# Hash attention and MLP mixer: keys and channels on the partitions, two heads side by side on the array, attention first and the mixer after it

## The chip, the cores and the metric

The kernel runs on one core of a Trainium2 chip. A core has a matrix engine (TensorE, PE in the profile; its loads of stationary operands are listed apart as PEld), VectorE (DVE), ScalarE (ACT), GpSimd (POOL), and SyncE (SP), which here only starts transfers. Matrix products read SBUF and write PSUM, which has eight banks of 512 float32 per partition. The metric is the time of one execution on the device, in microseconds.

## The reference

For 4 batches, 8 heads, 768 tokens and a head size of 64, each query attends to the keys whose six hash bits equal its own. The heads' outputs, side by side, are the input x (768 x 512) of a mixer with 256 hidden token units and 1536 hidden channels.

```python
q_bits = (einsum('bhsd,dk->bhsk', q, proj) > 0)      # k_bits likewise; 6 bits give a bucket
mask = q_bucket[:, :, :, None] == k_bucket[:, :, None, :]
scores = where(mask, (q @ k.T) / 8, -1e9)
scores = scores - max(scores, axis=-1, keepdims=True)
attn = exp(scores)
attn = attn / (sum(attn, axis=-1, keepdims=True) + 1e-9)
x = (attn @ v)                                       # (B, H, S, D) -> (B, S, H*D)

h = maximum(x.transpose(0, 2, 1) @ w_tok1, 0) @ w_tok2
u = x + h.transpose(0, 2, 1)
out = u + maximum(u @ w_ch1, 0) @ w_ch2
```

All is float32; the mixer's weights arrive as float64. q, k and v are normal numbers times 0.1.

## The kernel before

The work is written as steps, and a scheduler orders each engine's instructions from them. `run` interleaves two step generators: `attention_steps` of a batch beside `mixer_steps` of the batch before it (beside the first batch it is `double_weight_steps`, which converts the float64 weights in 20 chunks). The mixer of the last batch runs alone at the end.

A pair of heads shares the 128 partitions, 64 dimensions each. `prepare` turns q and k on TensorE, so that dimensions lie on the partitions (line 197, the helper `turn`), and computes the hash bits (line 215). `scores` takes 128 queries at a time: queries on the partitions, 768 keys along the row, one 1024-wide PSUM tile a head. A bfloat16 product of the scaled bits (line 233, 7 rows) adds 0 where all bits agree and a huge negative number elsewhere; the float32 product of q and k (line 239, 64 rows of the array a head) follows. VectorE takes the row's maximum (line 249), GpSimd scales it (253), ScalarE exponentiates and sums (256). `attend` turns the 128 x 768 weights, six blocks a head (197, copied out by 199 and 201), multiplies them with v (275: 128 queries stationary, 64 columns moving), and divides (280 to 282).

A float32 product is two instructions on TensorE, so counts in the profile are twice the program's; a transpose or a bfloat16 product is one.

The mixer has its token products at lines 319 and 330, a turn of u (197 again), and the channel products at 347 (384 columns) and 359 (512 columns). A weight chunk is a transfer and seven operations: four on VectorE (148, 152, 157, 160), two on GpSimd (163, 166), one more on VectorE (170).

Of the kernel before, what the change touches and what calls it, by code (L numbers as in the profile page):

```python
# [12 lines left out]
chip. Weights that come as float32 are loaded as they are.  # L13
"""
# [11 lines left out]
U32 = mybir.dt.uint32  # L26
I64 = mybir.dt.int64
ALU = mybir.AluOpType
ACT = mybir.ActivationFunctionType


@with_exitstack
def kernel(
    ctx: ExitStack,
    tc: tile.TileContext,
    q: bass.AP,
    k: bass.AP,
    v: bass.AP,
    proj: bass.AP,
# [8 lines left out]
    B, H, S, D = q.shape  # L48
    NB = proj.shape[1]
    DM = H * D  # L50
# [3 lines left out]
    NP = H // 2  # L54
# [3 lines left out]
    assert D == 64 and S == 6 * P and DM == 512 and NB <= 8 and H % 2 == 0  # L58
    assert DTOK % P == 0 and DCH % P == 0
    HALF = S // 2  # L60
    RH = NR // 2

    SCALE = 0.125
    MASKED = -1e9 / SCALE
    BIG = 2.0**62

    const = ctx.enter_context(tc.tile_pool(name="const", bufs=1))
    pool = ctx.enter_context(tc.tile_pool(name="sb", bufs=2))
    psum = ctx.enter_context(tc.tile_pool(name="ps", bufs=2, space=bass.MemoryType.PSUM))

# [4 lines left out]
    projblk = const.tile([P, 64], F32, name="projblk")  # L75
    nc.vector.memset(projblk, 0.0)
    for i in range(2):
        nc.sync.dma_start(out=projblk[D * i : D * i + D, 32 * i : 32 * i + NB], in_=proj)
    # Row NB has the bit -1/2 on both sides: -NB * BIG there cancels NB agreeing bits.
    bitscale = const.tile([64, 1], F32, name="bitscale")  # L80
    nc.gpsimd.memset(bitscale, BIG)
    for i in range(2):
        nc.gpsimd.affine_select(
            out=bitscale, in_=bitscale, compare_op=ALU.not_equal, fill=-NB * BIG,
            base=-(32 * i + NB), pattern=[[0, 1]], channel_multiplier=1,
        )

# [1 line left out]
    W1 = const.tile([P, NR, DTOK], F32, name="W1")  # L89
    W2 = const.tile([P, NJ, NR, P], F32, name="W2")  # L90
    WC1 = const.tile([P, NCB, DCH], F32, name="WC1")
    WC2 = const.tile([P, NHT, DM], F32, name="WC2")
# [7 lines left out]
    def words(w):  # L100
        return w.bitcast(U32) if double else w

    w1v = words(w_tok1).rearrange("(p r) c -> p (r c)", r=NR)
    w2v = words(w_tok2).rearrange("(j p) c -> p j c", p=P)
    wc1v = words(w_ch1).rearrange("(j p) c -> p j c", p=P)
    wc2v = words(w_ch2).rearrange("(t p) c -> p t c", p=P)
    W1f = W1.rearrange("p r c -> p (r c)")

    chunks = []
    for n in range(NR * DTOK // NW):  # L110
        chunks.append((w1v[:, NE * NW * n : NE * NW * (n + 1)], W1f[:, NW * n : NW * (n + 1)], None))
    for j in range(NJ):
        chunks.append((w2v[:, j], W2[:, j].rearrange("p r s -> p s r"), (S // NR, NR)))
    for j in range(NCB):
        for n in range(DCH // NW):
            chunks.append((
                wc1v[:, j, NE * NW * n : NE * NW * (n + 1)], WC1[:, j, NW * n : NW * (n + 1)], None,
            ))
    PER = 256
    for n in range(DM // PER):  # L120
        for t in range(NHT // 3):
            chunks.append((
                wc2v[:, 3 * t : 3 * t + 3, NE * PER * n : NE * PER * (n + 1)],
                WC2[:, 3 * t : 3 * t + 3, PER * n : PER * (n + 1)], (3, PER),
            ))

    def plain_weight_steps():
        for src, dst, shape in chunks:
            if shape == (S // NR, NR):
                raw = pool.tile([P, NW], F32, name="raw", tag="big", bufs=4)  # L130
                nc.gpsimd.dma_start(out=raw, in_=src)
                nc.vector.tensor_copy(dst, raw.rearrange("p (s r) -> p s r", r=NR))
            else:
                nc.gpsimd.dma_start(out=dst, in_=src)
            yield

    def double_weight_steps():
        for src, dst, shape in chunks:
            raw = pool.tile([P, NW, 2], U32, name="raw", tag="big", bufs=4)
            flat = raw.rearrange("p n w -> p (n w)")  # L140
            if len(src.shape) == 3:
                flat = flat.rearrange("p (t c) -> p t c", t=src.shape[1])
            nc.gpsimd.dma_start(out=flat, in_=src)
# [3 lines left out]
            # float32 with the high word's 20 bits of mantissa  # L147
# [8 lines left out]
            # the low word, in units of the number's signed power of two  # L156
# [3 lines left out]
            nc.vector.scalar_tensor_tensor(  # L160
                unit, lo, 2.0**-52, unit, op0=ALU.mult, op1=ALU.mult,
            )
            nc.gpsimd.tensor_tensor(big, big, unit, op=ALU.add)  # L163
            # what lies below float32's normal numbers is 0
            size = lo.bitcast(F32)
            nc.gpsimd.tensor_tensor(size, hi.bitcast(F32), hi.bitcast(F32), op=ALU.mult)  # L166
            if shape is not None:
                big = big.rearrange("p (a b) -> p a b", a=shape[0])
                size = size.rearrange("p (a b) -> p a b", a=shape[0])
            nc.vector.scalar_tensor_tensor(  # L170
                dst, size, LEAST * LEAST, big, op0=ALU.is_ge, op1=ALU.mult,
            )
            yield

# [1 line left out]
    def load_pair(b, hp):  # L176
        tiles = []
        for name, t in (("q", q), ("k", k)):
            nat = pool.tile([P, NR, 2, D], F32, name=f"{name}n", tag=f"{name}n")
            for i in range(2):  # L180
                nc.sync.dma_start(
                    out=nat[:, :, i], in_=t[b, 2 * hp + i].rearrange("(p r) d -> p r d", r=NR),
                )
            tiles.append(nat)
# [7 lines left out]
    def turn(dst, blocks, on_act):  # L192
# [3 lines left out]
        for i, block in enumerate(blocks):  # L196
            nc.tensor.transpose(ps[:, P * i : P * i + P], block, ident)  # L197
# [93 lines left out]
    def load_ahead(n):  # L291
        if n < len(pairs):
            loaded[pairs[n]] = load_pair(*pairs[n])
# [123 lines left out]
```

## Time and profile before

| | |
|---|---|
| three runs | 1546.4, 1555.5, 1544.23 us; median 1546.4 |
| span of the profiled execution, first to last instruction | 1543.2 us |
| what lies around the span | 3.2 us to the median, 1.0 us to the fastest run; the page has no time of its own for the profiled execution beside the span |
| busy, share of the span | PE 1482.8 us (96%), PEld 893.6 (58%), DVE 503.3 (33%), ACT 342.8 (22%), POOL 121.2 (8%) |
| transfers | 41.92 MB, mean 27 GB/s |

A busy share is an average over stages, and a matmul's end in the profile is modelled: an instruction is shown somewhat longer than the distance to the next one. What a matmul costs in a stream is read from the starts of its neighbours, or from a group's busy time divided by its count in a window where nothing else runs. PEclk is the share of TensorE's full clock that was granted.

### The profile page before, as it was taken

The page shows a single profiled execution, that of the slowest core. Times are in us where ns is not written, and L with a number is a line of the kernel's source. Part 1 is how long each engine was busy: PE and PEld are TensorE (multiplying, and loading weights), DVE is VectorE, ACT ScalarE, POOL GpSimd, SP SyncE. Part 2 cuts the span into 40 slices and gives each one's busy share as a digit, 9 for nine tenths or more (in the row PEclk, how much of TensorE's full clock was granted, in tenths as well). Part 3 has the DMA queues.
Part 4 walks back from the last instruction along what each step waited for, and adds up shares of the span by engine and source line. Part 5 has one row for each costly group of instructions (what it writes and reads, how often), then busy time and mean ns, then how long its engine had stood idle before and what let it go on. Part 6 is the DMA issues. An engine that isn't in the chain of part 4 may idle for free.

```text
span 1543.2 us, 15967 instructions
## 1 busy us (share of the span) xinstructions
PE 1482.8 (96%) x6560; PEld 893.6 (58%) x6560; DVE 503.3 (33%) x1141; ACT 342.8 (22%) x729; POOL 121.2 (8%) x261
## 2 busy tenths in 40 slices
PE   5999999899999999999999999999999999999998
PEld 2666656565656556654665556654566555655554
DVE  4455454623432323223432322223432232221000
ACT  1112122212332212212232122212223122211110
POOL 3223232300000000000000000000000000000000
PEclk7566565759999999999999999999999999999999
DMA  7122121101010101001010101001010000000000
GB/s 214 41 62 73 54 80 41 31 1 31 1 31 1 38 15 29 3 14 38 1 31 0 38 14 31 1 15 38 0 31 1 7 15 0 1 14 7 7 14 21
DMA packets 61609, 41.92 MB, mean 27 GB/s; under 512 B 51296, under 2 KB 55392, under 8 KB 61536
## 3 DMA queue, kind: packets, MB, share of 16 engines
q1 hardware_dynamic: 58144, 25.18, 6.1%
q0 software_dynamic: 3392, 15.73, 3.0%
q8 instruction: 51, 0.84, 0.2%
q14 instruction: 22, 0.18, 0.0%
HBM read 34.61 MB, written 6.29 MB: 27 GB/s over the span
## 4 chain that ended last, share of the span: by engine, by line
PE 89%; DVE 6%; issue 2%; POOL 1%; ACT 1%; DMA 0%; DVEq 0%; POOLq 0%; ACTq 0%
PE acc L275 19%; PE c L347 16%; PE c L359 16%; PE sc L239 15%; PE trp L197 11%; PE sc L233 5%; PE hp L215 3%; DVE e L249 3%; PE h L330 3%; PE t L319 3%; DVE eT L201 1%; POOL raw L166 0%; POOL tmp L163 0%; ACT e L256 0%; DMA raw<-in_moe_w_tok 0%
## 5 line engine op out<-in xcount | busy, mean ns | idle before, releaser
L275 PEld LDWEIGHTS acc<-vn,eT 128*128 128x128 f32 x2304 | 313.3, 220 | 7.7 <-issue 6.2
L275 PE MATMUL acc<-vn,eT 128*128 128x64 f32 x2304 | 317.3, 302 | 0.0
L249 DVE TENSOR_SCALAR_CACHE_REDUCE e<-sc 128x768 f32<-128x768 f32 x192 | 176.4, 955 | 347.8 <-PE sc L239 342.8
L256 ACT ACTIVATE e<-e,low 128x768 f32<-128x768 f32 x192 | 179.1, 933 | 461.5 <-POOL low L253 461.1
L359 PE MATMUL c<-WC,r 128*128 128x512 f32 x576 | 259.0, 595 | 0.0
L347 PE MATMUL c<-uT,WC 128*128 128x384 f32 x768 | 256.1, 489 | 0.0
L239 PE MATMUL sc<-kT,qT 64*128 64x512 f32 (+1 forms) x768 | 254.0, 587 | 0.0
L197 PE MATMUL trp<-ident,e 128*128 128x128 f32 x1152 | 194.6, 310 | 18.6 <-DVE eT L201 12.4
L197 PEld LDWEIGHTS trp<-ident,e 128*128 128x128 f32 x1152 | 140.7, 155 | 107.3 <-issue 46.0
L347 PEld LDWEIGHTS c<-uT,WC 128*128 128x128 f32 x768 | 143.3, 190 | 93.0 <-issue 1.9
L359 PEld LDWEIGHTS c<-WC,r 128*128 128x128 f32 x576 | 105.3, 190 | 111.9 <-issue 109.8
L239 PEld LDWEIGHTS sc<-kT,qT 64*128 64x128 f32 x768 | 94.0, 209 | 98.6 <-issue 93.9
L199 ACT COPY eT<-trp 128x384 f32<-128x384 f32 x192 | 90.1, 469 | 265.0 <-PE trp L197 261.8
L201 DVE COPY eT<-trp 128x384 f32<-128x384 f32 x192 | 106.4, 555 | 110.4 <-PE trp L197 110.1
L253 POOL TENSOR_SCALAR low<-top 128x1 f32<-128x1 f32 x192 | 42.1, 220 | 1101.9 <-DVE e L249 1101.8
L352 ACT ACTIVATE r<-c 128x384 f32<-128x384 f32 x96 | 47.1, 490 | 315.0 <-PE c L347 315.0
L233 PE MATMUL sc<-kb,qb 7*128 7x512 bf16 (+1 forms) x384 | 93.2, 356 | 18.8 <-DVE e L249 14.5
L282 DVE TENSOR_TENSOR x<-acc,den 128x128 f32<-128x128 f32 x96 | 27.9, 291 | 234.1 <-PE acc L275 234.1
L233 PEld LDWEIGHTS <-qb 7*128 7x128 bf16 x384 | 22.6, 93 | 117.6 <-issue 114.6
L366 DVE TENSOR_TENSOR o<-c,x 128x512 f32<-128x512 f32 x24 | 16.6, 691 | 177.4 <-PE c L359 177.4
L163 POOL TENSOR_TENSOR tmp<-tmp 128x768 f32<-128x768 f32 x20 | 36.1, 1803 | 109.0 <-DVE tmp L160 102.3
L330 PE MATMUL h<-r,W 128*128 128x512 f32 x96 | 44.2, 601 | 0.0
(45 smaller groups left out, 550.4 us busy)
## 6 DMA issues: line engine op xcount, KB each, us to landing
raw<-in_moe_w_ch POOLq DMA_DIRECT2D x16, 768.0 KB, 4.8
qn<-in_q SPq DMA_DIRECT2D x32, 192.0 KB, 3.3
kn<-in_k SPq DMA_DIRECT2D x32, 192.0 KB, 3.4
vn<-in_v SPq DMA_DIRECT2D x16, 384.0 KB, 3.2
out<-o SPq DMA_DIRECT2D x24, 256.0 KB, 2.0
raw<-in_moe_w_tok POOLq DMA_DIRECT2D x4, 768.0 KB, 7.5
projblk<-in_proj SPq DMA_DIRECT2D x2, 1.5 KB, 4.9
```

The costliest lines, as they stand in the source:

```text
L197: nc.tensor.transpose(ps[:, P * i : P * i + P], block, ident)
L199: nc.scalar.copy(dst, ps[:, : P * n])
L201: nc.vector.tensor_copy(dst, ps[:, : P * n])
L233: nc.tensor.matmul(ps[i][:, ks], qb[32 * i : 32 * i + NB + 1, qs], kb[32 * i : 32 * i + NB + 1, ks], start=True, stop=False,)
L239: nc.tensor.matmul(ps[i][:, ks], qT[D * i : D * i + D, qs], kT[D * i : D * i + D, ks], start=False, stop=True,)
L249: nc.vector.tensor_scalar(e, ps[i][:, :S], MASKED, None, op0=ALU.max, op1=ALU.max, accum_out=top[:, i : i + 1],)
L256: nc.scalar.activation(e, e, ACT.Exp, bias=low[:, i : i + 1], scale=SCALE, accum_out=sums[:, i : i + 1],)
L275: nc.tensor.matmul(acc[:, D * i : D * i + D], eT[i][:, P * c : P * c + P], vn[:, i, c], start=(i == 0 and c == 0), stop=(c == NR - 1), ski ...
L330: nc.tensor.matmul(ps, W2[:, j, r], r1[:, j], start=(j == 0), stop=(j == NJ - 1),)
L347: nc.tensor.matmul(ps[:, :HALF], WC1[:, cb, P * t : P * t + P], uT[cb // 2][:, cb % 2, sl], start=(cb == 0), stop=(cb == NCB - 1),)
L352: nc.scalar.activation(r2t, ps[:, :HALF], ACT.Relu)
L359: nc.tensor.matmul(ps, r2[t][:, P * c : P * c + P], WC2[:, t], start=(t == 0), stop=(t == NHT - 1),)
```

## The change

The program is rewritten. The host now hands in q and k already turned (`in_qk`, dimensions on the partitions), v in key chunks and a turned v as well; the output leaves with channels on the partitions and is turned back by the host.

- Scores have keys on the partitions: a tile is 128 keys x 2 heads x 384 queries, two PSUM banks. The two heads use rows 0 to 63 and 64 to 127 of the array. The bits are spread by small transfers to the same 64 rows a head, padded with zeros, so bits and scores have one shape.
- No maximum is subtracted: the exponential reads PSUM directly (masked scores become 0). `look` records the largest |q| and |k|; where it is above 2, a flag makes the kernel run `careful_attention` and the mixer a second time behind a branch.
- The weights need no turning: v is stationary (128 keys x 64), the exponentials move (384 queries), and the two heads write partitions 0 to 63 and 64 to 127 of one bank (columns of the array).
- Sums over keys: GpSimd and VectorE add the six tiles of a half (`collect`), a product with ones sums over the partitions, and `divide` also puts the mean of v where no key matched.
- x stays turned (`XT`, all batches). The mixer turns it back for the first token product (`turn`), keeps u with channels on the partitions, and takes 512 tokens at a time in `channels`.
- All attention comes first; then all of the mixer, with pools of its own. Within both, TensorE's order is the order in which the program is written; the scheduler orders the other engines. The channel weights are loaded and converted at the start of the mixer, 4 chunks a batch; the token weights during the first pairs of heads.

```diff
+        def product(t, c, first):                       # in scores(n, half, chunks)
+            for i in range(2):
+                rows = slice(D * i, D * i + D)
+                nc.tensor.matmul(                       # L232
+                    sc[c][:, i, :HALF], t[rows, 1, P * c : P * c + P], t[rows, 0, qs],
+                    start=first, stop=not first)
...
+                for c in chunks:
+                    product(qkt, c, True)
+                    product(bits, c, False)
+            for c in chunks:
+                e = pool.tile([P, 2, HALF], F32, name="e", tag="e", bufs=11)
+                nc.scalar.activation(e, sc[c][:, :, :HALF], ACT.Exp, scale=SCALE)   # L249
...
+        def weigh(n, acc, es, chunks):
+            for c, e in zip(chunks, es):
+                for i in range(2):
+                    nc.tensor.matmul(                   # L257
+                        acc[D * i : D * i + D, :HALF], vn[:, i, c], e[:, i],
+                        start=(c == 0), stop=(c == NR - 1))
...
+        def collect(es):
+            nc.gpsimd.tensor_tensor(a, es[0], es[1], op=ALU.add)       # L265
+            nc.gpsimd.tensor_tensor(a, a, es[2], op=ALU.add)           # L266
+            nc.vector.tensor_tensor(d, es[3], es[4], op=ALU.add)       # L268
+            nc.vector.tensor_tensor(d, d, es[5], op=ALU.add)           # L269
+            nc.vector.tensor_tensor(d, d, a, op=ALU.add)               # L270
...
+        def divide(n, half, num, es):
+            ps = psum.tile([P, 512], F32, name="sums", tag="sm", bufs=1)   # hashes uses "sm" too
+            for i in range(2):
+                nc.tensor.matmul(ps[D * i : D * i + D, :HALF], ones, es[:, i], ...)   # L278
+            # none, den, reciprocal, num on VectorE (L280, L282, L285, L286), XT on GpSimd (L290)
...
+        for n, half, g in groups:          # 16 pairs x 2 halves of the queries x 2 groups of 3 key chunks
+            es = scores(n, half, range(GR * g, GR * g + GR))
+            if held is not None:
+                step(held)                 # weigh of the group before; divide and collect by halves
+            held = (n, half, g, es)
+            if half == 0 and g == 0:
+                load(n + 3)
+                look(n + 1)                # L195 on VectorE, L198 on ScalarE
+            if half == 1 and g == 0 and n % 2 == 1:
+                hashes(n + 1)              # L207: bits of the next two pairs; 8 transfers, L218
+            if weights and n >= 2 and half == 0 and g == 1:
+                weights.pop(0)()           # a chunk of the token weights
...
+        turn(0)                            # mixer: L430
+        for b in range(B):
+            some_weights(4)                # L133 to L155, as lines 143 to 170 were
+            if b + 1 < B:
+                turn(b + 1)
+            mix1(b)                        # L440
+            if b:
+                mix2(b - 1)                # L452, its adds L458 on VectorE
+        mix2(B - 1)
...
+        for tt in range(B * S // TT):      # 6 x 512 tokens
+            channels(tt)                   # L466 (c1), L476 (c2)
...
+    run(attention)
+    run(mixer, True)
+    flag = nc.values_load(unsafe, min_val=0, max_val=1)
+    with tc.If(flag > 0):
+        run(careful_attention)
+        run(mixer, False)
```

On TensorE, in the middle of an attention stage, there stood before (sc are the scores, qb and kb the bits, trp the turned blocks of the exponentials e, acc the attention's output):

```order
L197 MATMUL trp<-ident,e 128x128 x6
L233 LDWEIGHTS qb
L233 MATMUL sc<-kb,qb 128x512
L233 LDWEIGHTS qb
L233 MATMUL sc<-kb,qb 128x256
L239 MATMUL sc<-kT,qT 128x512
L197 MATMUL trp<-ident,e 128x128 x6
L275 MATMUL acc<-vn,eT 128x64 x6
```

and there stands now, for one group (its last of three key chunks is shown, then the products with v of the group before and the sums):

```order
L232 MATMUL sc<-qk 128x384 x2
L232 LDWEIGHTS bits_98
L232 MATMUL sc<-bits_98 128x384
L232 LDWEIGHTS bits_98
L232 MATMUL sc<-bits_98 128x384
L257 MATMUL acc<-e,vn 64x384 x6
L278 MATMUL sums<-esd,ones 64x384 x2
```

The two heads' products were often apart (a single line 239 between bits and transposes); now each pair follows its partner, the transposes are gone, and the 64-column products have become 384 columns wide.

On VectorE, where the first weight chunks are converted, there stood before a chunk spread among the maxima and copies of the attention:

```order
L148 TENSOR_SCALAR tmp<-raw 128x768
L281 RECIPROCAL den<-den 128x2
L152 SCALAR_TENSOR_TENSOR tmp<-raw,tmp 128x768
L282 TENSOR_TENSOR x<-acc,den 128x128
L157 TENSOR_SCALAR tmp<-tmp 128x768
L160 SCALAR_TENSOR_TENSOR tmp<-raw,tmp 128x768
L249 TENSOR_SCALAR e,top<-sc 128x768 x2
L201 COPY eT<-trp 128x384 x2
L170 SCALAR_TENSOR_TENSOR WC_83<-raw,tmp 128x768
```

and now the four chunks of the token weights stand in the first halves of the attention, ahead of the sums (esd) that TensorE needs for them:

```order
L138 TENSOR_SCALAR tmp<-raw 128x768
L142 SCALAR_TENSOR_TENSOR tmp<-raw,tmp 128x768
L147 TENSOR_SCALAR tmp<-tmp 128x768
L150 SCALAR_TENSOR_TENSOR tmp<-raw,tmp 128x768
L268 TENSOR_TENSOR esd<-e 128x768
L155 SCALAR_TENSOR_TENSOR W_87<-raw,tmp 128x768
L269 TENSOR_TENSOR esd<-esd,e 128x768
L138 TENSOR_SCALAR tmp<-raw 128x768
L270 TENSOR_TENSOR esd<-esd,esa 128x768
L280 TENSOR_SCALAR none<-sums 128x384
```

A chunk now holds VectorE's queue while it waits for GpSimd ahead of line 155, and the additions for the sums wait behind it.

On VectorE in the mixer, where before the additions of line 333 stood among the attention's rows, there now stand the 16 chunks of the channel weights one after another, with the additions of the token mixing (line 458, which free PSUM banks) among them:

```order
L142 SCALAR_TENSOR_TENSOR tmp<-raw,tmp 128x768
L147 TENSOR_SCALAR tmp<-tmp 128x768
L458 TENSOR_TENSOR XT<-t_3072,XT 128x384
L150 SCALAR_TENSOR_TENSOR tmp<-raw,tmp 128x768
L458 TENSOR_TENSOR XT<-t_3076,XT 128x384
L458 TENSOR_TENSOR XT<-t_3080,XT 128x384
L155 SCALAR_TENSOR_TENSOR WC_2845<-raw,tmp 128x768
L458 TENSOR_TENSOR XT<-t_3084,XT 128x384
```

Four chunks stand ahead of the first addition, and the additions of batches 2 and 3 stand behind the twelfth.

More of the change, by code (lines that the diff above doesn't have):

```diff
@@ L47 @@
     P = 128
-    B, H, S, D = q.shape
+    B, NP, _, _, S = qk.shape
+    D = 64
     NB = proj.shape[1]
-    DM = H * D
+    DM = NP * P
     DTOK = w_tok1.shape[1]
@@ L192, in turn @@
[L192 to L211 removed]
+                to, size.rearrange("p (t n) -> p t n", t=rows), LEAST * LEAST,
@@ L371, in run @@
-    def run(main, n_main, side, n_side):
-        done = 0
-        for n, _ in enumerate(main, 1):
-            while side is not None and done < n * n_side / n_main:
-                if next(side, "end") == "end":
-                    side = None
-                done += 1
-        if side is not None:
-            for _ in side:
-                pass
-    N_ATT = NP * NR + 1
-    N_MIX = 2 * NJ + NR + NCB + 2 * (NHT + RH * 3)
-    load_ahead(0)
-    side, n_side = (double_weight_steps if double else plain_weight_steps)(), len(chunks)
@@ L386 @@
[L386 to L394 removed]
+                        ps, WC2[:, t, P * cb : P * cb + P], r2[t], start=(t == 0), stop=(t == NHT - 1),
+                    )
+                o = pool.tile([P, TT], F32, name="o", tag="o", bufs=3)
```

552 lines of the change are left out of this document (310 added, 242 removed).

## The prediction

> **What bounds the kernel now.** First the page's engine shares and the slices.
>
> ```profile
> span 1543.2 us, 15967 instructions
> PE 1482.8 (96%) x6560; PEld 893.6 (58%) x6560; DVE 503.3 (33%) x1141; ACT 342.8 (22%) x729; POOL 121.2 (8%) x261
> PEclk7566565759999999999999999999999999999999
> PE 89%; DVE 6%; issue 2%; POOL 1%; ACT 1%; DMA 0%; DVEq 0%; POOLq 0%; ACTq 0%
> ```
>
> TensorE is the bound: busy 96% of the span, and 89% of the chain that ended last. The fourth row says more: for the first nine slices it ran at about half its clock. Busy time by two windows puts numbers on it.
>
> ```profile
> core 0: us, PE busy (x) PEld busy (x) DVE busy (x) ACT busy (x) POOL busy (x), PEclk, DMA share, GB/s
> 0.00:360.00 360.00, 329.78 (x1246) 215.85 (x1247) 171.53 (x347) 74.24 (x155) 91.31 (x117) 0.61 0.22 65
> 360.00:1543.00 1183.00, 1153.02 (x5316) 677.78 (x5314) 331.77 (x795) 268.54 (x574) 29.91 (x144) 1.00 0.06 16
> ```
>
> While attention runs alone beside the weights the granted clock is 0.61; with mixer products among it, 1.00. So a shorter time needs less TensorE work, or a better clock early. The groups, shapes kept apart, show the work:
>
> ```profile
> L275 PE MATMUL acc<-vn,eT 128*128 128x64 f32 x2304 | 317.3, 302 | 0.0
> L359 PE MATMUL c<-WC,r 128*128 128x512 f32 x576 | 259.0, 595 | 0.0
> L347 PE MATMUL c<-uT,WC 128*128 128x384 f32 x768 | 256.1, 489 | 0.0
> L239 PE MATMUL sc<-kT,qT 64*128 64x512 f32 x384 | 201.7, 731 | 0.0
> L197 PE MATMUL trp<-ident,e 128*128 128x128 f32 x1152 | 194.6, 310 | 18.6 <-DVE eT L201 12.4 <-ACT eT L199 4.9 <-ACT e L256 0.7
> L239 PE MATMUL sc<-kT,qT 64*128 64x256 f32 x384 | 111.9, 443 | 0.0
> L233 PE MATMUL sc<-kb,qb 7*128 7x512 bf16 x192 | 64.7, 419 | 18.8 <-DVE e L249 14.5 <-DVE kb L220 4.2
> ```
>
> Transposes of the weights (195 us) exist only because queries lie on the partitions; the products with v move 64 columns a load, and cost 317.3/2304 = 0.138 us each.
>
> **Prices.** In the last stage only the channel products run (groups of the window 1425 to 1540):
>
> ```profile
> L359 PE MATMUL c<-WC,r 128*128 128x512 f32 x144 | 62.1, 592 | 0.0
> L347 PE MATMUL c<-uT,WC 128*128 128x384 f32 x163 | 52.9, 486 | 0.0
> ```
>
> A float32 pass (half of a product) of 512 columns costs 62.1/144 = 0.431 us, of 384 columns 52.9/163 = 0.325. The timeline of 700 to 712 shows what two heads side by side cost (start, length, count):
>
> ```profile
> 706.67 1.98 PE L319 MATMUL t<-x,W 128*128 128x512 f32 x4
> 708.59 0.50 PE L233 MATMUL sc<-kb,qb 7*128 7x512 bf16 x4
> 709.01 1.56 PE L239 MATMUL sc<-kT,qT 64*128 64x512 f32 x8
> 710.50 1.99 PE L319 MATMUL t<-x,W 128*128 128x512 f32 x4
> ```
>
> Four passes of 512 take 708.59 - 706.67 = 1.92, which is 4 x 0.431 plus **0.20 for the switch** to another shape of the array. The eight passes of line 239 (four of 512, four of 256 columns) would take 2.59 in turn; they took 1.49 with a switch, so 1.29: **row pairs run at once**. The four bit products (768 columns a head) took 0.42 with their switch: 0.21 for 384, for both heads.
>
> **The change, part by part.**
>
> *Attention on TensorE.* A group is three key chunks. Scores: 3 x (2 x 0.325 + 0.21) = 2.58. Products with v: 3 x 2 x 0.325 = 1.95, if the two heads, on columns of the array, also run at once. Two switches: 0.40. Sums: 0.65 in every second group, 0.33. Together 5.26; 64 groups: **336 us**. No row shows a column pair: its price lies between one pass (0.325) and two (0.65). I take one, by the row pair, the nearest row; in turn it would add 64 x 1.95 + 32 x 0.65 = 146, and some 31 in the hashes, whose four products sit on 32 columns each. The bits change type within one array shape, also not shown; 0.21 holds a switch already, so an end without it is about 20 us lower.
>
> *Hashes*, seven rounds in the flow: two halves of 0.65, 0.40 of switches, and, as `sm` is one bank, a wait for the copy of the first half, 0.75 by line 216's 0.55 (below) and two hops: 2.45 each, **17 us**. Their bits come back through transfers (3.3 us median from issue to landing for q, below), and the next pair's bits are due some 6 us after the last copy, so I add 1.5 us a round: **10 us**.
>
> *Start.* Before the hashes, 2.36 MB of two pairs must land.
>
> ```profile
> 0.00:40.00 40.00, 21.73 (x56) 9.12 (x57) 19.21 (x34) 6.61 (x12) 15.21 (x25) 0.74 0.71 207
> qn<-in_q SPq DMA_DIRECT2D x32, 192.0 KB, 3.3
> 22.81 0.82 PE L233 MATMUL sc<-kb,qb 7*128 7x512 bf16 x4 [4.24 <-DVE kb L220]
> ```
>
> At 207 GB/s that is 11 us after an issue at 1 to 2; hashes, copies and bit transfers behind pair 2's 1.6 MB make about **23 us**, as the first score product of before (22.81). I add **4 us** for 8 us at half clock.
>
> *Other engines.* Rows for their durations:
>
> ```profile
> L256 ACT ACTIVATE e<-e,low 128x768 f32<-128x768 f32 x192 | 179.1, 933 | 461.5 <-POOL low L253 461.1
> L281 DVE RECIPROCAL den<-den 128x2 f32<-128x2 f32 x96 | 15.7, 164 | 2.8
> L216 DVE TENSOR_SCALAR qb<-hp 64x384 bf16<-64x384 f32 x32 | 17.5, 548 | 62.9 <-PE hp L215 62.0
> L366 DVE TENSOR_TENSOR o<-c,x 128x512 f32<-128x512 f32 x24 | 16.6, 691 | 177.4 <-PE c L359 177.4
> L163 POOL TENSOR_TENSOR tmp<-tmp 128x768 f32<-128x768 f32 x20 | 36.1, 1803 | 109.0 <-DVE tmp L160 102.3 <-DVE den L281 3.5 <-DVE den L280 3.2
> 6.73 0.56 DVE L148 TENSOR_SCALAR tmp<-raw 128x768 uint32<-128x768 uint32 x1 [5.80 <-DMA raw<-in_moe_w_tok]
> 13.35 0.96 DVE L170 SCALAR_TENSOR_TENSOR W<-raw,tmp 128x768 f32<-128x768 f32 x1 [3.48 <-POOL raw L166]
> L280 DVE TENSOR_SCALAR den<-sums x96: 144/160/1467, 39.3 to 1372.8; 128x2 f32<-128x2 f32 x96
> ```
>
> A half of a pair is two groups, 10.5 us of TensorE. ScalarE: six exponentials of 0.93 and about 1.1 of copies and sums, 6.7: covered. GpSimd: two additions of 1.80 and a 0.9: 4.5, covered. VectorE: three additions of 0.96, three 384-wide operations of 0.55, the absolute maximum of 1536 columns every second half (0.8 a half), and a 384-wide reciprocal, which no row shows: two columns cost what other operations on two columns cost, so 0.55 at the low end; a few ns a column more are lost in that row, so up to 1.5. I take 1.0: together 6.3, or 6.7 with the hashes. Covered, with 3.8 us of slack. The sums are due a whole half after they are made.
>
> That cover fails once. A weight chunk holds VectorE from 6.73 to 13.35 + 0.96: 7.6 us, with GpSimd inside. Four of them stand among the first four halves: 30 + 4 x 6.3 = 55 us against 42 of TensorE, which waits for sums and for the bank they share with the hashes: **13 us**. Attention: 336 + 17 + 10 + 23 + 4 + 13 = **403**.
>
> *Mixer.* The columns are the same as before: 1152 passes of 512 in the channel products, 496.5; ahead of them 96 passes of 512 (41.4), 128 of 384 (41.6) and 96 transposes (13): 96 us. But the channel weights no longer load beside attention. VectorE works through 16 chunks in order, the first landing about 6 us into the mixer (5.4 us from issue to use at the start of before); twelve take 6 + 12 x 7.6 = 97 us, additions on the way about 4, and the additions of batch 2, which free the banks for batch 3's products, end with the thirteenth chunk, near 111. So the channel products start at **113** instead of 96: a new wait of 17 us. Mixer: 113 + 496.5 = **610**.
>
> *End.* The last addition 0.69, a store of about 2, the flag's load and the branch past the second pass: **4**. No |q| or |k| comes near 2, as 0.1 times a normal number would need 20 deviations; so the second pass costs only its branch, and a repeat is no rival.
>
> Sum: 403 + 610 + 4 = 1017 as a span, against 1543.2; the median of the runs lies 3.2 above the span, so **1020 us**.
>
> **A rule against the row.** The Trainium skill, TensorE: Matmul & The Clock Gate, Part 1, lets the gate open after one window of some 3.4 us of activity. Here the rows differ: 330 of 360 us were busy at a clock of 0.61. By the page, attention alone runs at full clock (my sum); the row makes a rival.
>
> **The rivals.**
>
> *Column pairs take turns.* 146 + 31 more, less some 25 of waits that then hide: about 1170. For it: no row shows such a pair. Against: row pairs do run at once. Chance 0.11.
>
> *VectorE becomes the bound in attention.* Line 280's two columns once took 1467 ns instead of 160, beside line 163 on GpSimd: the two can block each other. If each GpSimd operation holds VectorE for its whole length, a half costs 6.7 + 4.5 = 11.2, with a reciprocal of 1.5 11.7, against 10.5: 22 to 38 us more, about 1050. Chance 0.10. The Trainium skill, VectorE: DVE Perf Modes, First, the fixed hardware budget, gives the reciprocal a repeat count of 8: at its 0.96 GHz an estimate of 3.2 us for 384 columns; by that a half costs 8.9, still covered, or 13.4 with every hold, about 1110. No row here decides it, since two columns are too few.
>
> *The gate stays half shut through attention*, as in the first window: 336 + 17 twice, less hidden waits: about 1350. Against: then array work filled little of the time (products with v at 64 columns, waits for maxima); now over 85% streams. Chance 0.04.
>
> *Slower than before.* Pairs take turns in rows and columns alike, so half the array idles, and the gate stays shut on it. A group then has 3 x (1.30 + 0.42) + 3.90 + 0.65 + 0.40 = 10.1; with hashes 695 us, at half clock 1390; with 637 for the rest 2027. It passes 1546 below a clock of 695/909 = 0.76. Against: the row pairs above. Chance 0.02.
>
> **How the numbers follow.** The forecast, with its own spread, has 0.73: 965 to 1060 (down some 50 for the bits, the mixer's wait and the first halves; up 40 for waits between engines that the order only suggests). Range: 965 to 1175, which takes in the first two rivals and leaves out the last two and the edges. A measurement of this kernel tells about 1% from no change; no case lies within that: faster 0.97, same 0.01, slower 0.02.
>
> **What would show it.** Line 257: six pairs in about 2 us a group, starts together; if 3.9, the column rival. PEclk near 1 from the second slice on, else the gate. A TensorE wait near 60 us for line 282, and one near the mixer's start for line 458, confirm the two weight terms. Channel products at 0.43 a pass to the end. I am wrong if attention ends far from 400 us or the mixer takes other than about 610.

## The result, and the profile after

The changed kernel takes **1014.16 us** (median of 4 runs, 1010.47 to 1014.73) against 1550.95 for the kernel before beside it: a ratio of 0.6537, 95% interval 0.6506 to 0.6568. The forecast was 1020 us. The page is of the fastest of these runs, 1010.47 us (span, engines, granted clock by slices, chain by engine):

```profile
span 1008.7 us, 9010 instructions
PE 943.9 (94%) x3649; PEld 423.4 (42%) x3649; DVE 400.3 (40%) x425; ACT 240.7 (24%) x361; POOL 223.6 (22%) x153
PEclk9968999999999999989899999999999999999999
PE 69%; DVE 17%; POOL 6%; DMA 3%; issue 3%; ACT 2%; SPq 1%; DVEq 0%; POOLq 0%; ACTq 0%
```

TensorE's busy time fell by 538.9 us, the span by 534.5: all of the gain is time of TensorE, by less work and, in part, by a better clock. Its idle time hardly moved (60.4 us before, 64.8 now), but the fourth row shows that it now has other owners: VectorE has 17% of the chain, where it had 6%. The stages, by windows cut close to the first and last instruction of each:

```profile
core 0: us, PE busy (x) PEld busy (x) DVE busy (x) ACT busy (x) POOL busy (x), PEclk, DMA share, GB/s
0.00:20.40 20.40, 9.58 (x34) 2.77 (x34) 6.76 (x8) 4.83 (x9) 6.76 (x17) 1.00 0.61 235
20.40:395.20 374.80, 340.76 (x2142) 147.10 (x2142) 293.72 (x274) 175.93 (x250) 163.11 (x102) 0.95 0.20 66
395.20:508.80 113.60, 98.94 (x321) 54.72 (x321) 71.44 (x101) 17.00 (x32) 44.23 (x29) 0.94 0.34 111
508.80:1003.60 494.80, 494.66 (x1152) 218.80 (x1152) 27.70 (x43) 42.98 (x72) 9.45 (x6) 1.00 0.03 13
```

The rows are the start, attention, the mixer up to the channel products, and the channel products; 5.1 us follow. The groups of TensorE (busy us, mean ns) and two of VectorE:

```profile
L466 PE MATMUL c<-XT,WC 128*128 128x512 f32 x576 | 248.3, 592 | 0.6 <-DVE XT L458 0.6
L476 PE MATMUL c<-r,WC 128*128 128x512 f32 x576 | 248.2, 592 | 0.0
L232 PE MATMUL sc<-qk 64*128 64x384 f32 x768 | 168.9, 519 | 0.6 <-ACT e L249 0.6
L257 PE MATMUL acc<-e,vn 128*64 128x384 f32 x768 | 137.9, 494 | 0.0
L232 PE MATMUL sc<-bits 64*128 64x384 bf16 x384 | 65.4, 328 | 1.9 <-DMA bits<-g 1.9
L278 PE MATMUL sums<-esd,ones 128*64 128x384 f32 x128 | 26.8, 498 | 8.3 <-DVE den L282 8.3
L285 DVE RECIPROCAL den<-den 128x384 f32<-128x384 f32 x32 | 81.5, 2545 | 0.0
L155 DVE SCALAR_TENSOR_TENSOR W<-raw,tmp 128x768 f32<-128x768 f32 x4 | 8.0, 2006 | 9.8 <-POOL raw L154 9.8
```

Against the groups of before: the products with v take 137.9 us instead of 317.3, scores 168.9 instead of 313.6, bits 65.4 instead of 109.9; the transposes, 239.3 us with those of q, k and u, became 12.7, and sums cost 26.8. In the figures of before, 330 of the 1483 us were worked at a clock of 0.61. Two groups of attention in the timeline (start, length):

```profile
200.44 0.92 PE L232 MATMUL sc<-qk 64*128 64x384 f32 x4
...
203.06 2.16 PE L257 MATMUL acc<-e,vn 128*64 128x384 f32 x12
205.05 0.81 PE L278 MATMUL sums<-esd,ones 128*64 128x384 f32 x4
205.79 0.92 PE L232 MATMUL sc<-qk 64*128 64x384 f32 x4
...
206.71 0.81 PE L232 MATMUL sc<-qk 64*128 64x384 f32 x4
207.35 0.33 PE L232 MATMUL sc<-bits 64*128 64x384 bf16 x2
207.51 0.81 PE L232 MATMUL sc<-qk 64*128 64x384 f32 x4
...
210.50 0.85 PE L207 MATMUL hp<-qk,projblk 128*32 128x384 f32 x8
```

Twelve passes of line 257 take 205.05 - 203.06 = 1.99 us, that is 0.33 a pair: **column pairs run at once** (the first passes of the two heads start at 203.063 and 203.069). The waits of TensorE from 20 to 510 us (total, times, longest):

```profile
PE hp L207 <- DVE g L211: 14.2, 7, 5.1
PE hp L207 <- DVE den L282: 10.6, 1, 10.6
PE sums L278 <- DVE den L282: 8.3, 1, 8.3
PE t L452 <- DVE XT L458: 7.5, 1, 7.5
```

The two weight waits are there under the names that the prediction gave: line 282 (at 46 and 62 us, with 5.1 on line 211 just behind them) and line 458. The second ends at 495.85, late in the token mixing and not near the mixer's start, as the list at the prediction's end has it.

### The profile page after: what moved, and what is told of

Its sections match the earlier page's. It is cut to its first block, busy times and chain, and to the rows that moved or that the text cites. A ratio compares the mean times of both kernels' runs of the same rounds, so it can differ in the third digit from the quotient of the medians.

```text
span 1008.7 us, 9010 instructions
## 1 busy us (share of the span) xinstructions
PE 943.9 (94%) x3649; PEld 423.4 (42%) x3649; DVE 400.3 (40%) x425; ACT 240.7 (24%) x361; POOL 223.6 (22%) x153
## 4 chain that ended last, share of the span: by engine, by line
PE 69%; DVE 17%; POOL 6%; DMA 3%; issue 3%; ACT 2%; SPq 1%; DVEq 0%; POOLq 0%; ACTq 0%
PE c L466 25%; PE c L476 25%; PE sc L232 10%; PE acc L257 7%; POOL tmp L151 3%; POOL raw L154 2%; DVE den L285 2%; DVE tmp L150 2%; DMA qk<-in_qk 2%; DVE tmp L142 2%; ACT e L249 1%; DVE esd L269 1%; DVE esd L268 1%; PE sums L278 1%; PE hp L207 1%
## 5 line engine op out<-in xcount | busy, mean ns | idle before, releaser
L466 PE MATMUL c<-XT,WC 128*128 128x512 f32 x576 | 248.3, 592 | 0.6 <-DVE XT L458 0.6
L476 PE MATMUL c<-r,WC 128*128 128x512 f32 x576 | 248.2, 592 | 0.0
L249 ACT ACTIVATE e<-sc 128x768 f32<-128x768 f32 x192 | 151.9, 809 | 141.6 <-PE sc L232 141.1
L232 PE MATMUL sc<-qk 64*128 64x384 f32 x768 | 168.9, 519 | 0.6 <-ACT e L249 0.6
L466 PEld LDWEIGHTS c<-XT,WC 128*128 128x128 f32 x576 | 109.4, 190 | 138.4 <-issue 137.0
L476 PEld LDWEIGHTS c<-r,WC 128*128 128x128 f32 x576 | 109.4, 190 | 137.8 <-issue 137.8
L257 PE MATMUL acc<-e,vn 128*64 128x384 f32 x768 | 137.9, 494 | 0.0
L232 PEld LDWEIGHTS sc<-qk 64*128 64x128 f32 x768 | 68.1, 194 | 71.5 <-issue 60.5
L257 PEld LDWEIGHTS acc<-e,vn 128*64 128x64 f32 x768 | 49.5, 136 | 76.4 <-issue 75.5
L285 DVE RECIPROCAL den<-den 128x384 f32<-128x384 f32 x32 | 81.5, 2545 | 0.0
L232 PE MATMUL sc<-bits 64*128 64x384 bf16 x384 | 65.4, 328 | 1.9 <-DMA bits<-g 1.9
L268 DVE TENSOR_TENSOR esd<-e 128x768 f32<-128x768 f32 x32 | 39.1, 1223 | 33.5 <-ACT e L249 33.3
```

What stands on the lines that cost most here:

```text
L232: nc.tensor.matmul(sc[c][:, i, :HALF], t[rows, 1, P * c : P * c + P], t[rows, 0, qs], start=first, stop=not first,)
L249: nc.scalar.activation(e, sc[c][:, :, :HALF], ACT.Exp, scale=SCALE)
L257: nc.tensor.matmul(acc[D * i : D * i + D, :HALF], vn[:, i, c], e[:, i], start=(c == 0), stop=(c == NR - 1),)
L268: nc.vector.tensor_tensor(d, es[3], es[4], op=ALU.add)
L285: nc.vector.reciprocal(den, den)
L466: nc.tensor.matmul(ps, WC1[:, cb, P * t : P * t + P], XT[:, cb, sl], start=(cb == 0), stop=(cb == NCB - 1),)
```

## The experiments

The kernels of one session ran beside the kernel before; each median is told against 1014.16. The kernel before had medians from 1546.8 to 1551.0 in the five sessions, so a difference of some 4 us between sessions means nothing.

**Pairs of heads made unlike neighbours: loops turned round.** In both `scores` and `weigh`:

```diff
-for c, e in zip(chunks, es):
-    for i in range(2):
+for i in range(2):
+    for c, e in zip(chunks, es):
```

> After with the loops turned round in attention: the three key chunks of one head follow one another, then those of the other head (scores with their bits, and products with v), so neighbours on TensorE use the same half of the array. Nothing else is changed. Theory (the two heads ran at once, in rows and in columns): a group's scores go from 6 passes and 3 bits to 12 and 6 (+1.95 and +0.48 us), its v products from 6 passes to 12 (+1.9); 64 groups +278 us, or some 225 if at the seam from head to head the last product of the one still runs beside the first of the other; waits of up to 58 us may hide part: 1180 to 1290 us, granted clock still near 1 in attention. Rival (the heads never ran side by side, the gain came from elsewhere): no change, 1014. Second rival (a half-idle array shuts the gate): granted clock near 0.6 in attention and over 1500 us.

> After with only the products with v (line 257) turned round: three chunks of head 0, then three of head 1; scores as in after. Theory (column pairs ran at once): a group's v products go from 6 passes to 12 in turn, 2.0 to 3.9 us, or to 3.3 if one product overlaps at the seam; 64 groups +83 to +122 us, less up to 40 us of waits that then hide: 1055 to 1135 us. Rival (column pairs ran one after the other and only the row pairs gained): no change, 1014.

Measured: 1134.42 us (ratio to before 0.734, 0.7327 to 0.7353) with both turned, 1040.93 (0.6734, 0.6723 to 0.6746) with the products with v alone. Dearer, and in the direction of the theory, but below its ranges. The timeline of the first shows why:

```profile
202.74 2.85 PE L251 MATMUL acc<-e,vn 128*64 128x384 f32 x12
205.52 0.85 PE L207 MATMUL hp<-qk,projblk 128*32 128x384 f32 x8
```

The twelve passes took 2.78 us: neither 1.99 nor the 3.9 of one after the other. The six of one head need 1.95, and the second head's began 0.70 us in (203.44), beside the third of the first head's six. Turning the loops hides the pairing only in part; the test was too weak for the price, though it excludes "no change". The granted clock stayed at 1.00 from 100 to 390 us in this kernel, so an array half of which often idles did not shut the gate here.

**No pair possible.** Both heads' products with v on the same 64 columns:

```diff
-acc[D * i : D * i + D, :HALF], vn[:, i, c], e[:, i],
-start=(c == 0), stop=(c == NR - 1),
+acc[:D, :HALF], vn[:, i, c], e[:, i],
+start=(c == 0 and i == 0), stop=(c == NR - 1 and i == 1),
```

> After with the products of both heads with v (line 257) on the same 64 columns of the array, so that no two of them can run beside each other (they add into one result, which the copy puts in both halves: the work is the same, the values are not). Theory (column pairs ran at once and their worth is the 0.325 us of a second pass): 12 passes a group in 3.9 us instead of 2.0, 64 groups +122 us, of which some 20 to 35 hide waits for VectorE: 1100 to 1120. Rival (a pair's two passes shared the array's time and the second cost little anyway, or TensorE was waiting elsewhere): below 1050.

Measured: 1114.67 us (0.7193, 0.7154 to 0.7232), inside the theory's range. In its groups the line that took 137.9 us takes nearly twice as long:

```profile
L257 PE MATMUL acc<-e,vn 128*64 128x384 f32 x768 | 261.3, 490 | 0.0
```

In its timeline, products with v and sums together go from 205.79 - 203.06 = 2.73 to 208.02 - 203.36 = 4.66 us, six passes of 0.322 more:

```profile
203.36 3.76 PE L257 MATMUL acc<-e,vn 128*64 128x384 f32 x11
...
208.02 0.92 PE L232 MATMUL sc<-qk 64*128 64x384 f32 x4
```

The kernel also copies its result once more a half on ScalarE, but TensorE is busy 286.6 of the 290 us from 100 on and waits for none of it. The column pairs of line 257 are worth 100 us of this kernel; the forecast's price for them, 64 x 1.95 = 125 less what hides, holds.

**The bits on 7 rows**, so that the array changes shape at every product of bits:

```diff
-rows = slice(D * i, D * i + D)
+rows = slice(D * i, D * i + (D if first else NB + 1))
```

> After with the product of the bits on 7 rows of the array a head instead of 64 rows of which 57 hold zeros: the same columns, but another shape of the array at every product of bits. Theory (a switch of shape costs 0.1 to 0.2 us, and the 64 rows avoid it): a group has six switches more, +0.6 to +1.2 us, 64 groups +38 to +77 us: 1050 to 1090. Rival (switches cost nothing, and the 0.20 that the forecast took from before was the load of new weights): within 5 us of 1014.

Measured: 1043.48 us (0.6747, 0.6731 to 0.6763), 29 more, just under the range. The timeline of a chunk:

```profile
205.32 0.92 PE L232 MATMUL sc<-qk 64*128 64x384 f32 x4
206.17 0.34 PE L232 MATMUL sc<-bits 7*128 7x384 bf16 x2
206.43 0.92 PE L232 MATMUL sc<-qk 64*128 64x384 f32 x4
```

A chunk takes 206.43 - 205.32 = 1.11 us; in a run of like shape it takes about 0.81 (206.71 to 207.51 after the change). Two switches thus cost 0.30, or 0.15 each. TensorE is busy 990.7 us, 46.8 longer, of which some 11 fill former waits. The expectation counted six switches more a group; they are five, since the one from the last bits to the products with v was there before: 64 x 5 x 0.15 = 48, as measured. After the change, float32 and bfloat16 alternate in one shape at 0.64 us for the two float32 passes and 0.16 for the bits, so that change of type costs nothing that shows.

**The order of stages alone**, in the kernel before:

```diff
 for b in range(B):
     run(attention_steps(b, xs[b % 2]), N_ATT, side, n_side)
-    side, n_side = mixer_steps(b, x), N_MIX
+    side = None
+for b in range(B):
+    for _ in mixer_steps(b, xs[b % 2]):
+        pass
```

> Before with only the order of the stages changed: attention of all four batches first, then all of the mixer; layout and products as in before (two tiles hold the attention results in turn, so batches 2 and 3 overwrite those of 0 and 1: the work is the same, the values are not). Theory (it is the old form of attention that the clock is granted 0.61 for, and the order alone brings nothing): attention's TensorE work is some 900 us of busy time, a quarter of it at 0.61, so 194 us a batch at full clock; four at 0.61 with waits make about 1390, the mixer 590 more: near 1975, granted clock about 0.6 for the first 1400 us. Rival (the weights' conversions or the start held the clock down, not attention): 360 for the first batch, 205 for each other, 590 for the mixer: about 1565, clock 1.0 after 360 us.

Measured: a span of 1607.7 us (two runs, 1609.44 and 1646.02) against 1543.2. Both forecasts missed the time. The theory fell; of the rival, the clock came true. Windows of it:

```profile
0.00:350.00 350.00, 320.73 (x1179) 208.22 (x1180) 168.98 (x341) 72.45 (x151) 91.48 (x117) 0.60 0.22 66
350.00:784.00 434.00, 407.29 (x2554) 276.53 (x2553) 199.96 (x502) 143.38 (x309) 20.30 (x97) 0.98 0.10 25
784.00:860.00 76.00, 75.50 (x258) 49.88 (x258) 20.12 (x54) 16.73 (x36) 2.30 (x11) 0.53 0.03 6
860.00:1011.00 151.00, 143.74 (x937) 99.67 (x936) 71.14 (x181) 52.94 (x114) 7.54 (x36) 1.00 0.02 6
```

Attention of the old form runs at full clock from 350 us on, with no mixer beside it, except for one stretch of 76 us. So this form of attention does not by itself hold the clock down; whether the weights or the start did so up to 350 us was not separated. Nor does the order bring anything by itself: it costs 64.5 us of span, 36 of them at most in that one stretch. The gain lies in the rest of the rewrite, in less TensorE work above all. A part of it is clock: before, TensorE was busy 329.8 us at 0.61 in the first 360 us, which at full clock would be some 129 us less by an estimate; after, the 340.8 us of attention at 0.95 lose some 17. So about 110 of the 534 us are clock, and no run here shows which part of the rewrite opened it.

**What the weights cost: no conversion.** The seven operations of a chunk become one copy of the high words:

```diff
-nc.vector.tensor_scalar(big.bitcast(U32), hi, 3, 0x3FFFFFFF, ...)
...
+nc.vector.tensor_copy(to, hi.bitcast(F32).rearrange("p (t n) -> p t n", t=rows))
```

> After with one copy of the high words in place of the seven operations that convert a weight chunk (the conversion is left out, so the weights' values are not the true ones): VectorE holds about 1 us a chunk instead of 7.5, GpSimd nothing. Theory (the waits of TensorE of 8.3, 10.6 and 5.1 us before 80 us and the 17 us ahead of the channel products come from the conversions): attention's last product at about 373 instead of 394.5, channel products some 98 us later instead of 114: 972 to 982. Rival (the reciprocal or the bank shared by sums and hashes would make TensorE wait at these places anyway): above 995.

Measured: 975.14 us (0.6294, 0.6259 to 0.6328). Attention's last product ends at 375.5 us instead of 395.1, the channel products begin 97.8 after it instead of 113.8. The window between the two holds 94.8 us of TensorE work:

```profile
375.50:473.30 97.80, 94.76 (x323) 54.63 (x322) 34.38 (x53) 17.16 (x32) 2.27 (x2) 0.98 0.36 129
```

The weights' conversions cost 39 us by the medians (36 by the spans), and both weight terms of the forecast are real.

**Two buffers for the conversion.**

```diff
-tmp = pool.tile([P, 2, NW], F32, name="tmp", tag="cvt", bufs=1)
+tmp = pool.tile([P, 2, NW], F32, name="tmp", tag="cvt", bufs=2)
```

> After with two buffers instead of one for the conversion of a weight chunk, so that VectorE may begin the next chunk while GpSimd works on the last. Theory (the 17 us ahead of the channel products and part of the 24 us of TensorE waits between 46 and 80 us are VectorE standing behind GpSimd inside a chunk, 3.4 of 7.55 us): the period of a chunk in the mixer falls from 7.55 to about 4 to 5 us, the channel products start 95 to 100 us after attention's last product instead of 114, and attention loses up to 10 us of waits: 985 to 1000. Rival (landing of the chunks or the order of VectorE's instructions holds the mixer): period about 7.5 and 1010 to 1016.

Measured: 1028.73 us (0.6659, 0.6639 to 0.6679), **slower** by 14.6; both theories missed. Chunks with nothing between them did come faster, every 6.7 us instead of 7.55, but not every 4 to 5, and attention ended at 394.8 us, no earlier. The timeline of a chunk shows the first reason:

```profile
405.12 1.99 POOL L151 TENSOR_TENSOR tmp<-tmp 128x768 f32<-128x768 f32 x1 [3.32 <-DVE tmp L150]
405.48 2.44 DVE L142 SCALAR_TENSOR_TENSOR tmp<-raw,tmp 128x768 uint32<-128x768 uint32 x1
407.07 2.18 POOL L154 TENSOR_TENSOR raw<-raw 128x768 f32<-128x768 f32 x1
```

VectorE's line 142 takes 0.96 us alone and 2.44 here: it starts beside GpSimd's addition, which ends at 407.11, and ends 0.81 after that. GpSimd's line 154 takes 1.47 alone and 2.18 here. The two engines took turns; what the second buffer set side by side was paid back. This agrees with the Trainium skill, SBUF — State Buffer, Who interferes with whom, by which VectorE and GpSimd hold a shared pair of ports one at a time, for a whole instruction. The second reason is order: the scheduler now put fifteen chunks, not twelve, ahead of the first addition of batch 2 (line 458) on VectorE, and all sixteen ahead of the last ones; the channel products began 131 us after attention. How the 14.6 us divide between the two was not taken apart.

**VectorE held to the program's order**, in attention, in the mixer with a new order of chunks, and in both:

```diff
-        ) as psum, tc.manual_schedule(engines={PE}):
+        ) as psum, tc.manual_schedule(engines=pinned):        # {PE, DVE} where the text says so
...
-            some_weights(4)
+            some_weights(2)                                   # the mixer's new order
         mix2(B - 1)
+        steps.sort(key=lambda f: f.__defaults__[1])
+        some_weights(len(steps))
```

> After with VectorE in attention held to the order in which the program issues its work, so that the four weight chunks come one a pair of heads from the third pair on, instead of all four before 80 us. Theory (what cost TensorE 24 us was that four chunks of 7.5 us were crowded into the first halves; with 7.9 of 10.7 us busy a half, VectorE takes one chunk a pair with a wait of 2 us or less): attention's last product at about 378 instead of 394.5, all at 995 to 1002. Rival (each chunk costs TensorE its 6 us wherever it stands, as the sums behind it are late by so much): 1010 to 1016.

> After with the mixer's sixteen weight chunks placed otherwise: two instead of four ahead of each batch (the first channel weights), the eight of the second channel weights behind the last addition of line 458, those of its first 256 columns first; VectorE held to that order in the mixer. Theory (the channel products wait for additions that stand behind thirteen chunks on VectorE): with eight chunks ahead (60 us) TensorE's own 96 us set the start, the channel products begin some 100 us after attention's last product instead of 114: 998 to 1003. Rival (the second channel weights then come too late for line 476, or the landing of chunks holds the start): 1010 or more.

> Both of the two changes of order together. Theory (two separate waits, in attention and ahead of the channel products): the gains add, some 16 and 14 us: 980 to 988, close to the 975 of the kernel without conversions. Rival (the two gains are of one wait, or the pinned order costs elsewhere): no better than the better of the two.

Measured: 1077.05 (0.6959, 0.6949 to 0.6969), 1059.86 (0.6858, 0.6847 to 0.6869) and 1123.85 (0.7275, 0.7264 to 0.7286): all three slower, and their losses, not gains, add (62.9 + 45.7 = 108.6; measured 109.7). No theory's time was met. The second's rival had the size, but another reason; the third's, by which the pinned order costs elsewhere, came true. The waits of the first, then of the second:

```profile
PE hp L207 <- DVE g L211: 50.4, 7, 12.5
PE sums L278 <- DVE esd L270: 32.7, 22, 7.6
```
```profile
PE judge L499 <- DVE top L497: 60.9, 1, 60.9
```

In the first, the copy of the hashes (line 211) stands behind the additions of `collect` in the program: 5 us at the rounds without a chunk, 12.5 at the two with one; and sums wait 0.7 us in about half of the 32 halves, and 7.6 behind two of the chunks. So each of the four chunks, alone in its pair, costs TensorE some 7 us, about its length. The order as written is a worse one than the scheduler's. In the second, the mixer's products were done 96.2 us after attention, as wished, but the look at the largest |q| and |k|, which comes ahead of the channel products, now stood behind eight chunks.

**The mixer's order without that mistake**, and, on top of it, the token weights' chunks in the ring of q and k tiles:

```diff
             nc.vector.tensor_scalar(unsafe, one, SAFE, None, op0=ALU.is_gt)
+            steps.sort(key=lambda f: f.__defaults__[1])
+            some_weights(len(steps))
```
```diff
-raw = pool.tile([P, NW, 2], U32, name="raw", tag="raw", bufs=3)
+raw = pool.tile([P, NW, 2], U32, name="raw", tag=tag, bufs=bufs)    # attention: "qk", 5
```

> The mixer's order as in d2, but the look at the largest |q| and |k| (whose one transpose stands ahead of the channel products on TensorE) placed ahead of the eight late chunks instead of behind them; attention as in after. In d2 the last mixer product ended 96.2 us after attention, and TensorE then waited 60.9 us for that look. Theory (thirteen chunks ahead of the additions were the whole of the extra wait): channel products start some 98 us after attention's last product instead of 114, the eight late chunks (60 us) end in time for line 476: 995 to 1000. Rival (the late chunks now hold line 476, 41 us after line 466): 1005 or more.

> As d4, and in attention a weight chunk takes its buffer from the ring of the q and k tiles (five instead of four), so it cannot land, and so not be converted, before the pair of heads that it follows is done: the four chunks then stand one a pair on VectorE, from about 90 us on, and nothing is held to an order. Theory (crowding: a half leaves VectorE some 2.8 us, so a chunk of 7.5 is absorbed over a pair with at most 3 us of wait): 10 to 20 us better than d4, 978 to 988. Rival (each chunk costs TensorE its 6 us wherever it stands, as the sums are late by it): same as d4 within 4 us.

Measured: **997.95 us** (0.6433, 0.6409 to 0.6457) for the first, the best of the kernels that compute the whole; its interval does not touch that of the change. Its mixer before the channel products, by windows:

```profile
398.10:496.60 98.50, 94.82 (x320) 54.55 (x320) 54.57 (x78) 17.10 (x32) 27.84 (x18) 0.98 0.26 88
```

98.5 us instead of 113.6, with 94.8 of TensorE work at a clock of 0.98 where there were 98.9 at 0.94: the extra wait was that of the additions behind the chunks, with some 4 us of half clock. The second gives 1008.80 (0.6507, 0.6482 to 0.6532), 10.9 more, and both its theory and its rival (within 4 us) missed:

```profile
PE sc L232 <- ACT e L249: 18.3, 3, 9.1
PE hp L207 <- DVE den L282: 15.0, 2, 7.5
```

The chunks now stand one a pair, yet the four waits around them are 9.1, 7.5, 9.0 and 7.5 us. The first of them in the timeline of VectorE and ScalarE:

```profile
73.99 0.96 DVE L155 SCALAR_TENSOR_TENSOR W<-raw,tmp 128x768 f32<-128x768 f32 x1 [3.34 <-POOL raw L154]
...
79.33 1.75 DVE L195 TENSOR_REDUCE largest<-qk 128x1 f32<-128x1536 f32 x1 [2.45 <-DMA qk<-in_qk]
...
82.80 0.61 DVE L286 SCALAR_TENSOR_TENSOR num<-none,vsum,num 128x384 f32<-128x384 f32 x1
```
```profile
83.44 0.84 ACT L198 ACTIVATE vt<-vt 128x768 f32<-128x768 f32 x1 [11.21 <-DVE num L286]
84.29 1.49 ACT L249 ACTIVATE e<-sc 128x768 f32<-128x768 f32 x2
```

The chunk ends at 74.9; after two additions VectorE waits 2.5 us for a q and k tile to land (the ring that the chunk shares), and line 286 comes at 82.8. ScalarE's sum of v (line 198) waits 11.2 us for that, the exponentials stand behind it, and their banks hold TensorE. So here a chunk was not spread over the free moments of a pair. How much the shared ring adds was not taken apart; in the first of the two kernels line 195 also waits 1.7 to 3.1 us for its tile in every second pair from 138 us on, with no chunk near.

## Why the prediction was right

**The sum.** Attention ended at 395.1 us against 403 forecast, the channel products began 113.8 us later against 113 and ran 494.7 against 496.5, the end took 5.1 against 4: a span of 1008.7 against 1017. The total lies within 1% for reasons that partly cancel: groups and start were forecast too dear by some 17 us, the first chunks too cheap by 7 to 11.

*Groups*, 336 forecast. A group with sums takes 5.35 us (200.44 to 205.79), one without 4.71: 5.03 on the mean, 322 in all. Passes cost what the channel products said; the bits cost 0.16, not 0.21, since they no longer switch shape, as the forecast's lower end allowed.

*Column pairs*, the one price that no row showed: one pass, as taken. That was the nearest row and not a shown price, and it held. The rival that had 0.11 is excluded by the starts in the timeline and priced by the kernel on the same columns.

*Hashes and bits*, 17 and 10 forecast. Groups of the window 100 to 390 us:

```profile
L207 PE MATMUL hp<-qk,projblk 128*32 128x384 f32 x96 | 11.5, 556 | 9.0 <-DVE g L211 9.0
L232 PE MATMUL sc<-bits 64*128 64x384 bf16 x318 | 53.9, 324 | 0.7 <-DMA bits<-g 0.7
```

Six rounds cost 20.5 us, 3.4 each: 24 for seven, as every other round waits 2.3 us instead of 0.7 for the copy. The bits' return was almost wholly hidden: 0.7. Together 25 against 27.

*First chunks*, 13 forecast; TensorE waited 24, and without conversions attention ends 19.6 earlier. The mechanism is right, the term was mis-sized. The reciprocal was taken at 1.0 us and takes 2.545, outside the forecast's own ends of 0.55 and 1.5; VectorE then needs 7.9 us a half, not 6.3, and the forecast's own sum, 30 + 4 x 7.9 - 42, gives 20. And line 155 took 2.0 us among attention's work, 0.96 in the mixer. The Trainium skill, VectorE: DVE Perf Modes, First, the fixed hardware budget, was nearer: its repeat count of 8 gave the estimate of 3.2. The later experiments add a limit: four chunks close together cost TensorE 5 to 6 us each, by this sum because VectorE's free time takes up the rest; alone in a pair, each cost 7 to 9, and there the slack of 3.8 us a half was not to be had.

*Start*, 23 forecast, 20.5 measured (the first score product). With it the terms of attention make 391; the 4 us that are left are of the size that the forecast gave to half clock. *Mixer*: 113.8 against 113. The additions of batch 2 end behind the thirteenth chunk, at 506.6, which is 111.5 us after attention, where the forecast had 111. TensorE's longest wait, 7.5 us, ends already with the first of them, behind the twelfth chunk; in all it is idle for 14.7 us, and of its 98.9 us of work against 96 some 4 are half clock. Two experiments bear the term out: without conversions 97.8, with eight chunks ahead 98.5.

**VectorE as the bound.** From 20 to 395 us it is busy 294 of 375 us, the holds of GpSimd included (line 268 takes 1223 ns on the mean; line 270, the same operation once GpSimd is done, 958). The blocking is real, but 0.27 us a time and not the 1.85 of a whole GpSimd addition, and TensorE stayed the bound.

**The gate.** The forecast weighed a clock of 0.61 through all of attention at 0.04, because old attention "filled little of the time". The clock was 0.95, so the rival is out. The reason given is not supported: the old attention also got full clock after 350 us, and from 125 to 189 us the kernel before ran at 0.50 with TensorE shown busy 63.3 of 64 us. That the sum's full clock came true is luck as far as these runs show; what opens the gate stays open. The rival was also priced too high: at 0.61 the 353 us of groups and hashes grow by 226, which gives about 1245, and 1350 needs a clock near 0.5.

**Slower than before**: out, since pairs run at once in rows and in columns and the clock held.

## What to carry to other kernels

Where an operand of 64 rows or 64 columns leaves half of the array free, put an independent product of the same shape on the other half and next to it in order; look for starts a few ns apart (6 here). When TensorE work falls by a third, price the helpers anew, operation by operation: the waits that are left belong to engines that had been nobody's bound, and a long piece of work in such an engine's queue can cost its whole length (in attention a chunk of 7.5 us cost 5 to 9 in every place tried), until it is moved to a stretch where nobody waits. Ahead of an order by hand, list what else stands behind the moved piece on its queue: one small reduction cost 61 us.

## What the hardware showed that was not expected

- TensorE starts the other half's product while earlier ones still run, not only for the direct neighbour: twelve passes written three products a head at a time took 2.78 us, not 3.9, and the second head's first pass started when three of the first head's six were still to come.
- A reciprocal of 384 float32 columns takes 2545 ns on VectorE, where an operation with two tensors takes about 550 on as many.
- The granted clock stayed at 0.53 for 76 us in which TensorE shows 75.5 us busy, with old attention; after the change it was back at full rate within a few us of the waits near 80 us:

```profile
75.00:80.00 5.00, 0.58 (x4) 0.50 0.26 79
80.00:95.00 15.00, 15.00 (x94) 0.92 0.26 85
```

  The Trainium skill, TensorE: Matmul & The Clock Gate, Part 1, opens the gate after one busy window of some 3.4 us. The second row agrees with it; the 76 us do not, and no run here tells the two apart.
